# Batch 0's second half masked by multiplication, its gates reordered and one scaling moved to GpSimd, in an attention and SwiGLU kernel

## Chip, cores and metric

One core of a Trainium2 chip runs the whole program. The metric is the device time of one execution in microseconds, the median of several runs. Engines are named as in the profile: PE is TensorE, DVE is VectorE, ACT is ScalarE, POOL is GpSimd, SP is SyncE.

## What is computed

Windowed attention with a few global keys, and then a gated feed-forward block on its output. Batch is 4, heads 8, sequence 768, head size 64; keys 0 to 7 are global, and a query also sees the last 96 keys.

```python
scores = scale * q @ k.T - slope[h] * dist        # dist = 96 for a global key outside the window
a = softmax(where(is_global | is_local, scores, -1e9))
x = (a @ v) as [3072 tokens, 512]
g = x @ w_gate
out = (g / (1 + exp(-g)) * (x @ w_val)) @ w_out    # 512 -> 1536 -> 512
```

## The kernel before

The 3072 tokens are eight tiles of 384, two for each batch: tile 0 is the first half of batch 0, tile 1 its second half. For each batch the kernel makes queries and keys of head pairs transposed (qT, kT), scores by chunks of 120 keys, exponentials, then denominators and numerators for two quads of four heads, and from these x transposed (xT), four slabs of 128 features; quad g fills slabs 2g and 2g+1. For each tile the feed-forward part goes over 12 slices f of 128 hidden features: a gate (`gate_or_val(t, f, 0)`) and a value (`gate_or_val(t, f, 1)`), each four matmuls at L553, one for each slab of xT. The gate goes through tanh on ScalarE (L564) and a product on VectorE (L569, tile sl); the value is multiplied by that (L573) and gives hT. `out_part` multiplies three slices of hT by w_out (L585); four parts make 128 rows of the output.

Attention of the next half is woven into the feed-forward part of the tile before. The order is written out by hand: every engine runs its instructions in the order in which the Python code calls them. For tile 0 the list `tile0` (L805) holds gates, values and steps for the second half of batch 0; after it come the `stretches` (L813), which take each f of each tile with the steps that hang on it. Work that should wait a little is put on a list `later`, and `run_later(n)` (L255) takes n items off its head; the loop over `tile0` (L868) takes one before most gates and values, and all before a step.

There are two ways to put the position bias in. Batch 0 adds it before the exponential: `bias` (L340) multiplies a diagonal of the head's slope (slopeI) by the distances (dist), which starts the sum in PSUM, and `scores_half` (L351) adds the scores to it. The later batches multiply the exponential by a mask, exp(-slope * dist), which `make_masks` (L249) makes on ScalarE and `scores` (L375) applies on VectorE.

`both_values` (L506) makes denominators and numerators of a half for both quads, copies the numerators to SBUF on ScalarE (L518, tile ns) and puts four items on `later`: `spread_first` (the reciprocal denominators of quad 0 spread out, rb, and quad 0's two scalings), `spread` for quad 1 and its two scalings. A scaling is `scale_num` (L521, the instruction at L522): ns times rb gives a slab of xT. For batch 0 all four run on VectorE; for later batches quad 0's two run on GpSimd.

GpSimd also issues nearly all loads (weights, keys, queries, values), in the order of the calls from L611 to L700. Its issues wait for earlier transfers by semaphores of eight, used in turn. The loads of the last lines are w_out in four parts (`load_wo`, L215), batch 1's keys and queries (`load_qk`, L149), the global rows (`load_globals`, L177) and batch 1's values in seven chunks (`load_v_rest`, L167). PSUM banks are handed out in turn by `bank` and `spare`; `widen` (L847) gives tile 0's last slices four more of them, `narrow` takes these back in tile 1.

Of the kernel before, what the change touches and what calls it, by code (L numbers as in the profile page):

```python
# [37 lines left out]
def kernel(  # L38
# [110 lines left out]
    def load_qk(b, h0, h1):  # L149
        for st, src in ((kst[b], k), (qst[b], q)):  # L150
            nc.gpsimd.dma_start(
                out=st[:, h0:h1, :],
                in_=src[b, h0:h1].rearrange("h (p j) d -> p h (j d)", p=128))
# [13 lines left out]
    def load_v_rest(b, c):  # L167
        n = min(KC, S - KC * c)
        nc.gpsimd.dma_start(  # L169
            out=vSs[b][NG:NG + n, c, :, :],  # L170
            in_=v[b, :, KC * c:KC * c + n, :].rearrange("h p d -> p h d"))
# [5 lines left out]
    def load_globals():  # L177
        for dst, src in ((kG, k), (vG[:, 1:], v)):
            nc.gpsimd.dma_start(
                out=dst.rearrange("p b h d -> p (b h) d"),  # L180
                in_=src[1:, :, 0:NG, :].rearrange("b h p d -> p (b h) d"))

    def copy_globals(b, c0=0):
        nc.sync.dma_start(
            out=vSs[b][0:NG, c0:],
            in_=vG[:, b, :, :].unsqueeze(1).broadcast_to([NG, NCH - c0, H, D]))
# [28 lines left out]
    def load_wo(g):  # L215
        nc.gpsimd.dma_start(
            out=wo[:, 3 * g:3 * g + 3, :],
            in_=moe_w_out[384 * g:384 * g + 384].rearrange("(f p) d -> p f d", p=128))
# [26 lines left out]
    def single(name, tag, dt=FP32):  # L245
        return ps.tile([128, 512 if dt == FP32 else 1024], dt, name=name, tag=tag)
# [13 lines left out]
    class Pair:  # L260
# [87 lines left out]
                        start=(col == 0), stop=False, skip_group_check=True)  # L348
            return sc

        def scores_half(self, half, which, sc, put_off=False):  # L351
            hp = self.hp
            for c, col, q0, n in SCORES[half, which]:
                for hi in range(2):
                    r = slice(64 * hi, 64 * hi + 64)
                    nc.tensor.matmul(  # L356
                        sc[hi][:, col:col + n],
                        lhsT=self.kT[r, 128 * c:128 * c + 128],
                        rhs=self.qT[r, q0:q0 + n], start=False, stop=True,
                        skip_group_check=True)  # L360
            c, col, q0, n = SCORES[half, which][-1]
            at = sb2.tile([128, 2, BANK], FP16, name="at", tag=f"at{half + which}", bufs=NP)
            self.at[half, which] = at

            def exps():
                for hi in range(2):
                    nc.scalar.activation(out=at[:, hi, 0:col + n], in_=sc[hi][:, 0:col + n],  # L367
                                         func=AF.Exp, scale=scale)

            if put_off:  # L370
                later.append(exps)
            else:
                exps()

        def scores(self, bk, mul_eng, sc):  # L375
            hp = self.hp
# [129 lines left out]
    def both_values(b, half):  # L506
        two = [quads[b, g] for g in range(2)]
        for quad in two:
            den = spare("den") if b > 0 else bank("den")
            quad.weigh(half, den, None)  # L510
            quad.invert(den)
        srcs = {}
        for g, quad in enumerate(two):
            for side in range(2):
                num = spare("num") if b == 0 and g == 1 else bank("num")
                quad.weigh(half, num, side)
                src = sb2.tile([128, TB], FP32, name="ns", tag="ns", bufs=4)
                nc.scalar.copy(out=src, in_=num[:, 0:TB])  # L518
                srcs[g, side] = src

        def scale_num(eng, g, side):  # L521
            eng.tensor_mul(two[g].x_out(half, side), srcs[g, side], two[g].rb)  # L522

        def spread_first():
            two[0].spread()
            for side in range(2):
                scale_num(nc.gpsimd if b > 0 else nc.vector, 0, side)

        later.append(spread_first)
        def spread():  # L530
            two[1].spread()

        later.append(spread)
        for side in range(2):
            def scale(side=side):
                scale_num(nc.vector, 1, side)

            later.append(scale)
# [19 lines left out]
    def gate_or_val(t, f, which, c0=0):  # L558
        products(t, f, which, c0, NC)
        dst = gv.pop((f, which))  # L560

        if which == 0:
            th = sb2.tile([128, TB], FP32, name="th", tag="th")
            nc.scalar.activation(out=th, in_=dst[:, 0:TB], func=AF.Tanh, scale=0.5)  # L564
            if t == 0 and f < 4:
                sl = sb2.tile([128, TB], FP32, name="sl", tag="ns", bufs=4)
            else:
                sl = sb2.tile([128, TB], FP32, name="sl", tag="sl")
            nc.vector.scalar_tensor_tensor(  # L569
                out=sl, in0=th, scalar=1.0, in1=dst[:, 0:TB], op0=AluOp.add, op1=AluOp.mult)  # L570
            gv["sl", f] = sl
        else:
            nc.vector.tensor_mul(hTs[t][:, f, :], dst[:, 0:TB], gv.pop(("sl", f)))  # L573
# [82 lines left out]
    p_tr(1, "x2", "o0", A)  # L656
    V(out=vG[:, 0], in_=vG32)
    V(out=vSs[0][0:NG, 0:4], in_=vG[:, 0].unsqueeze(1).broadcast_to([NG, 4, H, D]))
    copy_globals(0, 4)
    load_w(wg, 0)  # L660
    load_half(1, 0, 4)
# [21 lines left out]
    quads[0, 1].denominators(single("den", "o0"))  # L683
    for side, tag in enumerate(("x2", "x0")):
        quads[0, 1].numerators(side, single("num", tag))

    load_w(wg, 8)
    for c in range(3, NCH):
# [1 line left out]
    load_w(wv, 8)  # L690
    load_wo(0)
    load_wo(1)
    load_wo(2)
    stage(1)
    load_qk(1, 0, 4)
    load_globals()
    load_wo(3)
    load_qk(1, 4, 8)
    for c in range(NCH):
        load_v_rest(1, c)  # L700

    gv["n"] = 1
    hb = [bank("gps") for _ in range(4)]
# [1 line left out]
    def first_gates(*terms):  # L705
        for c, f in terms:
            products(0, f, 0, c, c + 1, hb[f])
# [20 lines left out]
    def vas(b, half):  # L728
        return lambda: both_values(b, half)
# [18 lines left out]
    def sch(hp):  # L748
        def step():
            p = pairs[0, hp]  # L750
            scs = [p.bias(1, 0), p.bias(1, 1)]
            for which in range(2):
                p.scores_half(1, which, scs[which], which == 1 and hp != 1)
        return step

    def fetch(b, *hps):
# [41 lines left out]
    def first_val(f):  # L798
        return lambda: products(0, f, 1, 0, 2)

    V(out=dist[:, 2 * WIN:2 * WIN + 168], in_=dist[:, WIN:WIN + 168])
    V(out=dist[:, 2 * WIN + 168:], in_=dist[:, WIN:WIN + 48])
    first_gates(*[(c, f) for f in range(4) for c in range(2)])
    first_gates((2, 0), (2, 1), (2, 2), (3, 0), (3, 1), (2, 3), (3, 2), (3, 3))
    tile0 = [(0, 0), (1, 0), (2, 0), (3, 0), trh(0, 1, True), first_val(0), first_val(1),  # L805
             bias_of(0, 0), bias_of(0, 1), scores_of(0), (0, 1), (1, 1), (2, 1),
             trh(2, 3, False), sch(1), (3, 1), (4, 0), sch(2), (5, 0), (4, 1), (5, 1),
             (6, 0), (6, 1), sch(3), (7, 0), (7, 1), (8, 0), vas(0, 1), (8, 1)]

    def ff(t, f0, f1, n_out=(0,)):  # L810
        return [(t, f, n_out[(f - f0) % len(n_out)]) for f in range(f0, f1)]

    stretches = [  # L813
        (ff(0, 9, 10) + ff(0, 10, 12, (1,)), {}),
        (ff(1, 0, 6, (1, 0, 0, 1, 1, 2)) + ff(1, 6, 10, (1, 1, 1, 0)) + ff(1, 10, 12, (2,)), first(1, 1)),
        (ff(2, 0, 12, (1,)) + ff(3, 0, 12, (1,)), both(2, 1)),
        (ff(4, 0, 12, (1,)) + ff(5, 0, 12, (1,)), both(4, 2)),
        (ff(6, 0, 12, (1,)), second(6, 3)),
# [7 lines left out]
    def mask_at(t, f, which, h, c0, c1):  # L826
        after.setdefault((t, f, which), []).append(lambda: make_masks(h, c0, c1))

    spots = [(0, f) for f in (8, 9, 10, 10, 11, 11)] + [(1, f // 2) for f in range(10)]
    for n, (t, f) in enumerate(spots):  # L830
        mask_at(t, f, n % 2, n // 2, *((0, WIN), (WIN, 3 * WIN))[n % 2])
    at_step(1, 7, lambda: [copy_globals(b) for b in range(1, B)])
    for b, base, rate, v_at in ((2, 20, 2.0, (31, 32, 33, 34, 35, 36, 37)), (3, 38, 1.4, (56, 57, 58, 59, 60, 61, 62))):
        items = [(base, lambda b=b: stage_rows(b)), (base + 1, lambda b=b: load_ends(b))]
# [10 lines left out]

    outs = [(t, i, part) for t in range(NT - 1) for i in range(3) for part in range(4)]
    def widen():  # L847
        run_later(len(later))
        x, n = state["x"], gv["n"]
        state["x"] = ([state["tags"][(state["n"] + i) % 4] for i in range(4)]  # L850
                      + [x[(n + i) % 3] for i in range(3)])
        gv["n"] = 0
# [4 lines left out]
        state["n"] += 3  # L857
        gv["n"] = 0

    at_step(0, 9, widen)  # L860
    at_step(1, 2, narrow)

    def take(step_list):
# [3 lines left out]

    for item in tile0:  # L868
        if callable(item):
            take([item])  # L870
            continue
        f, which = item
        if item not in ((5, 0), (8, 1)):
            run_later(1)
        gate_or_val(0, f, which, (NC if f < 4 else 0, 2 if f < 2 else 0)[which])
        for fn in after.pop((0, f, which), []):
            fn()
# [61 lines left out]
```

## Time and profile before

| | |
|---|---|
| runs | 240.0, 240.38, 240.97 us; median 240.38 |
| the profiled execution | 241.65 us, of which the span from the first to the last instruction is 239.9 |
| clock granted to TensorE | 0.998 |
| transfers | 25.00 MB, mean 104 GB/s |
| VectorE sl, L569 | 96 instructions, mean 551 ns |
| ScalarE tanh, L564 | 96 instructions, mean 495 ns |
| scaling, L522, on VectorE and on GpSimd | 14 with median 554 ns, 10 with median 996 ns |

The profile gives for each engine its busy time, for each line and operation the number and mean time of its instructions, and the chain of waits that ended last. A timeline row has the start in microseconds from the span's start, the length, engine, line, operation, output and inputs, how many instructions were merged (x), and in brackets how long the engine stood idle before it and what ended that.

### The profile page before, as it was taken

To read this page: it belongs to the slowest core of one execution; us is meant where nothing else is said; L and a number is where in the kernel's file an instruction comes from. 1 tells how busy PE (TensorE), PEld (TensorE's weight loads), DVE (VectorE), ACT (ScalarE), POOL (GpSimd) and SP (SyncE) were. 2 spreads that over 40 slices of the span, in tenths; PEclk is the share of its full clock that TensorE was granted. 3 is DMA by queue.
4 is the path that set the end of the run, shared out by engine and by line. 5 is a ranking of instruction groups with operands and counts; after the bars stand their busy time and mean duration, and the time that the engine had idled before them with its cause. 6 is when DMAs were issued, how large, how long until landed. Compare 5 with 4: busy or idle time off the path is not lost.

```text
span 239.9 us, 6040 instructions
## 1 busy us (share of the span) xinstructions
PE 234.5 (98%) x2424; PEld 136.0 (57%) x2424; DVE 167.9 (70%) x363; ACT 128.0 (53%) x290; POOL 94.1 (39%) x113
## 2 busy tenths in 40 slices
PE   8999999999999999999999999999999999999994
PEld 4566565656555556555655556555655556555543
DVE  6688659978897678776786668776785668555530
ACT  4647775888855374376356364376356435233311
POOL 8886575668960002995072152700031223000000
PEclk9999999999999999999999999999999999999999
DMA  7999999999998538999139849930110110111022
GB/s 131 159 201 201 188 197 204 196 166 160 159 133 127 123 84 118 115 134 120 45 61 107 120 107 136 119 63 0 48 44 3 44 44 3 46 45 44 3 87 87
DMA packets 83333, 25.00 MB, mean 104 GB/s; under 512 B 72601, under 2 KB 80361, under 8 KB 83305
## 3 DMA queue, kind: packets, MB, share of 16 engines
q0 software_dynamic: 64208, 14.05, 64.0%
q1 hardware_dynamic: 18664, 10.36, 18.0%
q8 instruction: 19, 0.31, 0.6%
q10 hardware_dynamic: 432, 0.21, 0.3%
q14 instruction: 10, 0.07, 0.1%
HBM read 28.62 MB, written 6.29 MB: 146 GB/s over the span
## 4 chain that ended last, share of the span: by engine, by line
PE 92%; DMA 3%; DVE 2%; POOL 1%; ACT 1%; issue 0%; DVEq 0%; ACTq 0%; POOLq 0%
PE gps L553 26%; PE vps L553 26%; PE ops L585 25%; PE num L445 4%; PE sc L385 3%; DMA q<-in_q_dram 3%; PE den L445 2%; PE sc L345 2%; PE trs L272 1%; PE ops L601 1%; PE sc L356 1%; POOL k L118 1%; DVE sl L569 1%; DVE xT L503 1%; PE trs L298 1%
## 5 line engine op out<-in xcount | busy, mean ns | idle before, releaser
L564 ACT ACTIVATE th<-gps 128x384 f32<-128x384 f32 x96 | 47.4, 495 | 62.6 <-PE gps L553 56.6
L569 DVE SCALAR_TENSOR_TENSOR sl<-th,gps 128x384 f32<-128x384 f32 x96 | 52.8, 551 | 38.3 <-ACT th L564 37.7
L553 PE MATMUL gps<-xT,wg 128*128 128x384 f16 x384 | 78.0, 327 | 0.3 <-DVE xT L503 0.3
L553 PE MATMUL vps<-xT,wv 128*128 128x384 f16 x384 | 77.8, 326 | 0.0
L585 PE MATMUL ops<-wo,hT 128*128 128x512 f16 x276 | 73.1, 379 | 0.0
L573 DVE TENSOR_TENSOR hT<-vps,sl 128x384 f16<-128x384 f32 x96 | 53.0, 554 | 8.2 <-PE vps L553 0.5
L553 PEld LDWEIGHTS <-wg 128*128 128x128 f16 x384 | 35.6, 98 | 31.7 <-issue 2.1
L553 PEld LDWEIGHTS <-wv 128*128 128x128 f16 x384 | 37.2, 98 | 25.2
L585 PEld LDWEIGHTS <-hT 128*128 128x128 f16 x276 | 26.9, 98 | 23.7
L393 ACT ACTIVATE at<-sc 128x432 f16<-128x432 f32 x72 | 33.8, 533 | 10.2 <-PE sc L385 10.2
L522 POOL TENSOR_TENSOR xT<-ns,rb 128x384 f16<-128x384 f32 x10 | 9.8, 996 | 66.4 <-ACT ns L518 35.1
L169 POOL DMA_DIRECT2D vS<-in_v_dram x28 | 24.7, 891 | 5.3 <-DMA kst<-in_k_dram 1.9
L591 ACT ACTIVATE osb<-ops 128x512 f32<-128x512 f32 x23 | 13.7, 597 | 14.6 <-PE ops L585 14.4
L404 POOL TENSOR_TENSOR at<-at,masks 128x864 f16<-128x864 f16 x4 | 7.3, 1825 | 23.9 <-ACT at L393 19.3
L404 DVE TENSOR_TENSOR at<-at,masks 128x864 f16<-128x864 f16 x20 | 12.2, 610 | 5.6 <-ACT at L393 5.6
L518 ACT COPY ns<-num 128x384 f32<-128x384 f32 x24 | 9.8, 493 | 9.6 <-PE num L445 9.6
L192 POOL DMA_DIRECT2D kst<-in_k_dram x16 | 14.0, 886 | 1.8 <-DMA qst<-in_q_dram 1.1
L192 POOL DMA_DIRECT2D qst<-in_q_dram x16 | 13.7, 876 | 0.3 <-issue 0.3
L367 ACT ACTIVATE at<-sc 128x432 f16<-128x432 f32 (+2 forms) x32 | 11.5, 449 | 2.9 <-PE sc L356 2.9
L401 DVE TENSOR_TENSOR at<-at,masks 128x432 f16<-128x432 f16 x24 | 8.1, 378 | 4.3 <-ACT at L393 4.3
L445 PE MATMUL num<-at,vS 128*32 128x216 f16 (+6 forms) x576 | 10.9, 224 | 0.0
L455 DVE STREAM_TRANSPOSE dT<-den 128x384 f32<-128x384 f32 x16 | 9.3, 581 | 1.2 <-PE den L445 0.5
(71 smaller groups left out, 168.0 us busy)
## 6 DMA issues: line engine op xcount, KB each, us to landing
out_dram<-osb SPq DMA_DIRECT2D x23, 256.0 KB
vS<-in_v_dram POOLq DMA_DIRECT2D x24, 120.0 KB, 6.4
wg<-in_moe_w_gate_dram POOLq DMA_DIRECT2D x6, 256.0 KB, 8.8
wv<-in_moe_w_val_dram POOLq DMA_DIRECT2D x6, 256.0 KB, 7.7
wo<-in_moe_w_out_dram POOLq DMA_DIRECT2D x4, 384.0 KB, 9.3
qst<-in_q_dram POOLq DMA_DIRECT2D x16, 96.0 KB, 5.1
kst<-in_k_dram POOLq DMA_DIRECT2D x16, 90.0 KB, 5.4
kst<-in_k_dram POOLq DMA_DIRECT2D x2, 384.0 KB, 11.1
```

The costliest lines, as they stand in the source:

```text
L169: nc.gpsimd.dma_start(out=vSs[b][NG:NG + n, c, :, :], in_=v[b, :, KC * c:KC * c + n, :].rearrange("h p d -> p h d"))
L192: nc.gpsimd.dma_start(out=st[b][p0:p0 + n, h // 2, :, h % 2, :], in_=src[b, h, 0:n * J].rearrange("(t p) d -> p t d", p=n))
L367: nc.scalar.activation(out=at[:, hi, 0:col + n], in_=sc[hi][:, 0:col + n], func=AF.Exp, scale=scale)
L393: nc.scalar.activation(out=at[:, hi, :], in_=sc[hi][:, 0:BANK], func=AF.Exp, scale=scale)
L404: mul_eng.tensor_mul(at, at, m[:, :, o:o + BANK])
L445: nc.tensor.matmul(dst[r, o:o + n], lhsT=ones[:, 0:32] if side is None else vals[:, 4 * g + j, side::2], rhs=pairs[b, 2 * g + j // 2].at[c ...
L553: nc.tensor.matmul(gv[f, which][:, 0:TB], lhsT=w[:, c, 128 * f:128 * f + 128], rhs=x_of(t)[:, c, :], start=(c == 0), stop=(c == NC - 1))
L564: nc.scalar.activation(out=th, in_=dst[:, 0:TB], func=AF.Tanh, scale=0.5)
L569: nc.vector.scalar_tensor_tensor(out=sl, in0=th, scalar=1.0, in1=dst[:, 0:TB], op0=AluOp.add, op1=AluOp.mult)
L573: nc.vector.tensor_mul(hTs[t][:, f, :], dst[:, 0:TB], gv.pop(("sl", f)))
L585: nc.tensor.matmul(ops, lhsT=hTs[t][:, f, 128 * i:128 * i + 128], rhs=wo[:, f, :], start=(f == 0), stop=(f == NFF - 1))
L591: nc.scalar.mul(out=osb, in_=ops, mul=0.5)
```

## The change

Five things are changed, and the loop is fitted to them.

- Pairs 1 to 3 of batch 0's second half (`sch`) no longer call `bias`. Their score matmuls start the sum themselves, and each exponential is followed by multiplications with a mask on VectorE: two for the first part of a half (72 and 192 columns of two heads), one for the second (432 columns of two heads). Pair 0 (`bias_of`, `scores_of`) stays.
- The masks that this needs, columns WIN to 3*WIN of heads 2 to 7, are made before tile 0's first tanh; the two copies that extend dist stand further ahead. The remaining masks keep their number and get other places.
- Gates and values of tile 0 stand in another order, the list now reaches to the tile's end, two output parts are in it, and three later ones change places in tile 1. The tile sl gets three buffers. `widen` is called after `both_values` and no longer empties `later`.
- Quad 0's two scalings of batch 0's second half go to GpSimd.
- The third and fourth part of w_out, the global rows, the second half of batch 1's keys and queries and its values are called in a step of `tile0`, `late_widen`, which stands after `vas(0, 1)` and ahead of gate 10.

```diff
-        def scores_half(self, half, which, sc, put_off=False):
+        def scores_half(self, half, which, sc, put_off=False, masked=False):
...
-                        rhs=self.qT[r, q0:q0 + n], start=False, stop=True,
+                        rhs=self.qT[r, q0:q0 + n], start=masked, stop=True,
...
+            def mask():
+                for a, d0, m in BIAS[half, which]:
+                    a2 = at[:, :, a:a + m]
+                    nc.vector.tensor_mul(a2, a2, masks[:, 2 * hp:2 * hp + 2, d0:d0 + m])
...
+            if masked:
+                later.append(mask)
...
-                scale_num(nc.gpsimd if b > 0 else nc.vector, 0, side)
+                scale_num(nc.gpsimd, 0, side)
...
-                sl = sb2.tile([128, TB], FP32, name="sl", tag="sl")
+                sl = sb2.tile([128, TB], FP32, name="sl", tag="sl", bufs=3)
...
+    V(out=dist[:, 2 * WIN:2 * WIN + 168], in_=dist[:, WIN:WIN + 168])
+    V(out=dist[:, 2 * WIN + 168:], in_=dist[:, WIN:WIN + 48])
     copy_globals(0, 4)
...
+    for h in range(2, H):
+        make_masks(h, WIN, 3 * WIN)
...
-    load_wo(2)
     stage(1)
     load_qk(1, 0, 4)
-    load_globals()
-    load_wo(3)
-    load_qk(1, 4, 8)
-    for c in range(NCH):
-        load_v_rest(1, c)
+
+    def late_loads():
+        load_wo(2)
+        load_globals()
+        load_wo(3)
+        load_qk(1, 4, 8)
+        for c in range(NCH):
+            load_v_rest(1, c)
...
-            scs = [p.bias(1, 0), p.bias(1, 1)]
             for which in range(2):
-                p.scores_half(1, which, scs[which], which == 1 and hp != 1)
+                p.scores_half(1, which, banks("sc"), which == 1 and hp != 1, True)
+            if hp != 1:
+                later.insert(0, later.pop(1))
...
+    def late_widen():
+        late_loads()
+        widen()
+
+    def out_next():
+        out_part(*outs.pop(0))
+
     tile0 = [(0, 0), (1, 0), (2, 0), (3, 0), trh(0, 1, True), first_val(0), first_val(1),
              bias_of(0, 0), bias_of(0, 1), scores_of(0), (0, 1), (1, 1), (2, 1),
-             trh(2, 3, False), sch(1), (3, 1), (4, 0), sch(2), (5, 0), (4, 1), (5, 1),
-             (6, 0), (6, 1), sch(3), (7, 0), (7, 1), (8, 0), vas(0, 1), (8, 1)]
+             trh(2, 3, False), sch(1), (3, 1), (4, 0), (5, 0), sch(2), (6, 0), (4, 1), (5, 1),
+             (6, 1), sch(3), (7, 0), (7, 1), (8, 0), (9, 0), vas(0, 1), late_widen, (10, 0), (8, 1),
+             (11, 0), (9, 1), (10, 1), out_next, (11, 1), out_next]
...
-        (ff(0, 9, 10) + ff(0, 10, 12, (1,)), {}),
-        (ff(1, 0, 6, (1, 0, 0, 1, 1, 2)) + ff(1, 6, 10, (1, 1, 1, 0)) + ff(1, 10, 12, (2,)), first(1, 1)),
+        (ff(1, 0, 6, (0, 0, 0, 1, 2, 2)) + ff(1, 6, 10, (1, 1, 1, 0)) + ff(1, 10, 12, (2,)), first(1, 1)),
...
-        run_later(len(later))
         x, n = state["x"], gv["n"]
...
     for item in tile0:
         if callable(item):
-            take([item])
+            if item is not late_widen and item is not out_next:
+                run_later(len(later))
+            item()
             continue
         f, which = item
-        if item not in ((5, 0), (8, 1)):
+        if item == (8, 1):
+            run_later(3)
+        elif item not in ((6, 0), (7, 0)):
             run_later(1)
```

More of the change, by code (lines that the diff above doesn't have):

```diff
@@ L799, in first_val @@
         return lambda: products(0, f, 1, 0, 2)
-    V(out=dist[:, 2 * WIN:2 * WIN + 168], in_=dist[:, WIN:WIN + 168])
-    V(out=dist[:, 2 * WIN + 168:], in_=dist[:, WIN:WIN + 48])
     first_gates(*[(c, f) for f in range(4) for c in range(2)])
     first_gates((2, 0), (2, 1), (2, 2), (3, 0), (3, 1), (2, 3), (3, 2), (3, 3))
+    def late_widen():
[3 more added lines that the diff above has]
+        out_part(*outs.pop(0))
     tile0 = [(0, 0), (1, 0), (2, 0), (3, 0), trh(0, 1, True), first_val(0), first_val(1),
              bias_of(0, 0), bias_of(0, 1), scores_of(0), (0, 1), (1, 1), (2, 1),
-             trh(2, 3, False), sch(1), (3, 1), (4, 0), sch(2), (5, 0), (4, 1), (5, 1),
-             (6, 0), (6, 1), sch(3), (7, 0), (7, 1), (8, 0), vas(0, 1), (8, 1)]
+             trh(2, 3, False), sch(1), (3, 1), (4, 0), (5, 0), sch(2), (6, 0), (4, 1), (5, 1),
+             (6, 1), sch(3), (7, 0), (7, 1), (8, 0), (9, 0), vas(0, 1), late_widen, (10, 0), (8, 1),
+             (11, 0), (9, 1), (10, 1), out_next, (11, 1), out_next]
     def ff(t, f0, f1, n_out=(0,)):
@@ L827, in mask_at @@
         after.setdefault((t, f, which), []).append(lambda: make_masks(h, c0, c1))
-    spots = [(0, f) for f in (8, 9, 10, 10, 11, 11)] + [(1, f // 2) for f in range(10)]
-    for n, (t, f) in enumerate(spots):
-        mask_at(t, f, n % 2, n // 2, *((0, WIN), (WIN, 3 * WIN))[n % 2])
+    for h, (t, f) in enumerate(((0, 9), (0, 10), (0, 11), (1, 0), (1, 1), (1, 2), (1, 3), (1, 4))):
+        mask_at(t, f, 1, h, 0, WIN)
+    for h, f in ((0, 10), (1, 11)):
+        mask_at(0, f, 0, h, WIN, 3 * WIN)
     at_step(1, 7, lambda: [copy_globals(b) for b in range(1, B)])
@@ L858, in narrow @@
         gv["n"] = 0
-    at_step(0, 9, widen)
     at_step(1, 2, narrow)
```

## Prediction

> **What bounds the kernel now.** I read the page's busy shares and chain first, then TensorE's timeline around the end of tile 0, then GpSimd's timeline over the same stretch.
>
> ```profile
> PE 234.5 (98%) x2424; PEld 136.0 (57%) x2424; DVE 167.9 (70%) x363; ACT 128.0 (53%) x290; POOL 94.1 (39%) x113
> ...
> PE 92%; DMA 3%; DVE 2%; POOL 1%; ACT 1%; issue 0%; DVEq 0%; ACTq 0%; POOLq 0%
> ```
>
> TensorE is busy for 98% of the span and carries 92% of the chain that ends last. So every microsecond of matmul removed shortens the kernel, and every microsecond in which TensorE waits lengthens it. The question is whether a new wait appears. TensorE's timeline (start, length, line, operation) at the border of tiles 0 and 1:
>
> ```profile
> 40.24 0.81 PE L553 MATMUL vps<-xT,wv 128*128 128x384 f16 x4
> 40.89 0.81 PE L585 MATMUL ops<-wo,hT 128*128 128x512 f16 x3
> 41.53 0.81 PE L553 MATMUL gps<-xT,wg 128*128 128x384 f16 x4
> 42.18 0.81 PE L553 MATMUL vps<-xT,wv 128*128 128x384 f16 x4
> ```
>
> Four products take 0.65 us from start to start (40.24 to 40.89) and nothing stands between groups. The row at 41.53 is the first gate of tile 1, the first reader of the x of batch 0's second half (xT, written at L522). Its four matmuls read quad 0 (c = 0, 1) and quad 1 (c = 2, 3); VectorE had finished all four scalings at 40.56. Now GpSimd, whose queue issues the loads:
>
> ```profile
> 31.16 0.77 POOL L216 DMA_DIRECT2D wo<-in_moe_w_out_dram  x1 [0.16 <-DMA vS<-in_v_dram]
> 32.57 0.80 POOL L151 DMA_DIRECT2D kst<-in_k_dram  x1 [0.64 <-DVE hT L573]
> 33.59 0.75 POOL L151 DMA_DIRECT2D qst<-in_q_dram  x1 [0.22 <-ACT th L564]
> 34.83 0.68 POOL L179 DMA_DIRECT2D kG<-in_k_dram  x1 [0.49 <-issue]
> ...
> 36.16 0.78 POOL L216 DMA_DIRECT2D wo<-in_moe_w_out_dram  x1
> 37.43 0.81 POOL L151 DMA_DIRECT2D kst<-in_k_dram  x1 [0.49 <-DMA wo<-in_moe_w_out_dram]
> 39.34 0.75 POOL L151 DMA_DIRECT2D qst<-in_q_dram  x1 [1.09 <-DMA wo<-in_moe_w_out_dram]
> 41.30 0.95 POOL L169 DMA_DIRECT2D vS<-in_v_dram  x1 [1.21 <-DMA wo<-in_moe_w_out_dram]
> 43.24 0.94 POOL L169 DMA_DIRECT2D vS<-in_v_dram  x1 [1.00 <-DMA kst<-in_k_dram]
> 45.27 3.59 POOL L169 DMA_DIRECT2D vS<-in_v_dram  x4 [1.09 <-DMA qst<-in_q_dram]
> 49.47 0.64 POOL L169 DMA_DIRECT2D vS<-in_v_dram  x1 [0.61 <-DMA kst<-in_k_dram]
> ```
>
> GpSimd is late: it issues batch 1's last load at 49.47 and is free at 50.11, 8.6 us after TensorE has begun tile 1. The brackets show why: before most issues it waits for an earlier transfer to land, while the page's DMA row stands at 9 tenths in every slice from 6 to 72 us. The queue runs as fast as the transfers let it, and the place of a load in the program's text doesn't slow it or speed it.
>
> [...] L522 took 996 ns on GpSimd and 554 on VectorE, 1.8 times. [...] Here GpSimd's pool configuration is changed (two records of 44 ns) at 70.2, ahead of its first L522, but that L522 then waited for ScalarE until 94.4, so this trace neither shows nor excludes the price. [...]
>
> ```profile
> 4.38 1.19 PE L345 MATMUL sc<-dist,slopeI 128*128 128x432 f16 x6
> ...
> 11.05 0.70 PE L345 MATMUL sc<-dist,slopeI 128*128 128x432 f16 x6
> ```
>
> The same six matmuls cost 1.19 us early and 0.70 later. No long idle of TensorE stands in the trace[...].
>
> **The change, part by part.**
>
> *Bias matmuls of pairs 1 to 3 go.* Each pair had six at L345: 0.70 us from start to start for pair 1 (23.77 to 24.47), 0.69 for pair 2 (26.19 to 26.88), 0.69 for pair 3 (30.58 to 31.27). TensorE saves 2.08 us, and reaches tile 1's first gate at 41.53 - 2.08 = 39.45 if nothing in tile 0 stalls.
>
> *Mask multiplications come* on VectorE, three a pair. L404 has 610 ns for 864 elements and L401 378 for 432; the line through both gives 223 ns for 2x72 and 352 for 2x192. A pair costs 223 + 352 + 610 = 1.19 us, three 3.56. Two scalings leave (2 x 0.554 = 1.11): net 2.45 us more. From 20 to 40 us VectorE is busy 7.60 + 7.26 = 14.9 of 20, so 5.1 us are free. Bounds: nothing, or up to 2.45 us of delay to TensorE in tile 0. I take nothing, for the reason under the fourth part: a delay of tile 0 of less than 18 us is hidden there. Without that cover it would cost up to 2.45.
>
> *Six masks earlier on ScalarE* stand between the last exp and the first tanh, where it idles 3.41 us (14.69 to 18.10). A 432-wide mask is 0.55 and neighbours overlap by about 0.10 (0.38 + 0.55 alone, 0.83 as a pair), so six take 6 x 0.55 - 5 x 0.10 = 2.8. The two copies of dist (0.19 and 0.17) move into VectorE's 1.22 us of idle before 10.18. Both cost nothing; uncovered they would be hidden like the masks. Gate order, PSUM rotation, the third sl buffer and the shifted output parts keep the counts on TensorE; their new waits lie in tile 0 or leave the sum of tile 1 alone. Two output parts precede tile 1 before and after. Cost nothing, with the same cover.
>
> *Quad 0's scaling moves to GpSimd, and this decides.* The step that holds the late loads runs directly after the step that only puts the scaling on the list of postponed work. The scaling is taken off that list at the next gate. So the built program's order on GpSimd is: third wo load, kG, vG, fourth wo, second kst and qst, seven vS loads, a library reload, and only then the two scalings. The late loads are ahead of the scaling, not behind it, as the summary has it. Tile 1's first two matmuls each wait for GpSimd, and all of TensorE's queue stands behind them.
>
> When is GpSimd free? All issues before the scaling are those of before with the third wo moved behind kst and qst: the same bytes, and the last vS issue again waits for the second kst load. I take 50.11. Even if no load waited, the 13 issues take 0.77 + 0.68 + 0.66 + 0.78 + 0.81 + 0.75 + 0.95 + 0.94 + 3.59 + 0.64 = 10.57 us after about 33.4 (34.34, the end of the qst issue, less the third wo's 0.77 and 0.16): 44.0, still after 39.45. The reload has no row[...]. A gain is excluded, since an instruction is added. [...] The two scalings take 1.96 together (a pair at 94.43); add 0.1 for the signal. [...]
>
> *What follows.* Before, from that second matmul (41.53 + 0.16 = 41.69) to the end of the span took 239.9 - 41.69 = 198.2 us of dense TensorE work, and none of it is removed. TensorE will have stood still for 57.1 - 39.45 = about 18 us, and I let it restart at half rate for 4 us, which costs half of that, 2.0; bounds 0 (the clock doesn't fall) and 4.4 (as in this trace's start, where the slow rate lasted from 1.2 to about 10). The loads for batch 2, queued behind the scaling, come 8 us later, but their readers come 18 later.
>
> The sum: 58.12 + 198.2 + 2.0 = 258.3 us of span, against 239.9. The profiled execution took 241.65, 1.75 more than its span, but the median of the runs, 240.38, lies 0.48 above that span. On the median's footing: 258.8.
>
> **Rivals.** *The reload costs nothing.* For it: its records are 44 ns, and the first scaling of before took no longer than the other nine (992 to 1001 ns). Against: those had 24 us of idle in front. Then 58.12 falls to 52.17 and the median to 252.8.
>
> *The scaling goes in time (the other side).* If GpSimd came to the scaling by 39.45 - 1.96 - 0.1 = 37.4, for instance because the loads truly stood behind it, TensorE wouldn't wait and only the bias saving would stay: 240.38 - 2.08 = 238.3. Against it stands the built order, and the 10.57 us of issue work. The point from which it decides is 37.4 against 50.11.
>
> *A longer wait.* [...]
>
> **How the numbers follow.** Forecast (reload paid) 0.52, reload free 0.34, longer wait 0.09, in time 0.04, something that lands within 0.5% 0.01. The predicted time is 258.8. The range starts at the free reload less 1.5 for a clock that stays up or loads that land earlier, 251.3, and ends at 261.5, which leaves out the tail of the longest wait and the fast case. A difference under 0.5%, 1.2 us, is about what a measurement of this kernel cannot tell from no change. Slower 0.95, within it 0.01, faster 0.04.
>
> **What would show it.** On TensorE: the first gate of tile 1 reached near 39.5, its first matmul at about 57 (51 if the reload is free) waiting for GpSimd's xT. On GpSimd: the last vS issue ending near 50[...], then two scalings of about 1.0. Matmuls after the gap about 320 ns apart instead of 163 for some 4 us. From there to the end 198 us plus 2. No L345 rows for pairs 1 to 3. I am wrong if GpSimd's scaling stands before the late loads, or those are issued by 37.

## The result and the profile after

The changed kernel takes 254.53 us (median of four runs, 254.2 to 254.78), against 240.5 us for the kernel before (four runs beside it): 1.058 times as long, 95% interval 1.056 to 1.061. The profiled execution took 254.57 us, and its span is 252.8.

The page of the changed kernel: busy shares, TensorE's row and its clock row of the 40 slices (6.3 us each, in tenths), and the chain that ended last by engine.

```profile
PE 234.7 (93%) x2406; PEld 135.3 (54%) x2406; DVE 169.2 (67%) x370; ACT 127.7 (51%) x290; POOL 95.9 (38%) x115
...
PE   8799995079999999999999999999999999999995
...
PEclk9999999569999999999999999999999999999999
...
PE 78%; DMA 15%; POOL 5%; issue 1%; ACT 0%; POOLq 0%
```

TensorE has as many busy microseconds as before (234.7 against 234.5, although 18 matmuls are gone), but 93% of a longer span instead of 98%. One slice of its row, from 44 to 51 us, is 0, and in the chain DMA and POOL have taken 20% together. The clock row, all 9 before, has a 5 and a 6 at the same place.

TensorE's timeline of the changed kernel, from the last work of tile 0 to the first gates and values of tile 1:

```profile
40.48 0.81 PE L592 MATMUL ops<-wo,hT 128*128 128x512 f16 x3
51.55 0.48 PE L560 MATMUL gps<-xT,wg 128*128 128x384 f16 x1 [10.27 <-POOL xT L529]
52.50 1.12 PE L560 MATMUL gps<-xT,wg 128*128 128x384 f16 x3 [0.47 <-POOL xT L529]
53.42 1.48 PE L560 MATMUL vps<-xT,wv 128*128 128x384 f16 x4
54.70 0.96 PE L560 MATMUL gps<-xT,wg 128*128 128x384 f16 x4
55.49 0.81 PE L560 MATMUL vps<-xT,wv 128*128 128x384 f16 x4
```

The first gate of tile 1 waits 10.27 us for the first scaling on GpSimd, and its second matmul 0.47 us more for the second. Then the four products of a value take 1.28 us from start to start (53.42 to 54.70), where four took 0.65 before: the half clock. At 55.49 they are back at about 0.65. GpSimd in the same kernel:

```profile
45.45 3.58 POOL L169 DMA_DIRECT2D vS<-in_v_dram  x4 [0.99 <-DMA wo<-in_moe_w_out_dram]
49.76 0.64 POOL L169 DMA_DIRECT2D vS<-in_v_dram  x1 [0.73 <-DMA kst<-in_k_dram]
50.50 1.95 POOL L529 TENSOR_TENSOR xT<-ns,rb 128x384 f16<-128x384 f32 x2
```

The last load of batch 1 is issued until 50.40, and the scalings follow at 50.50. From the third part of w_out, at 33.52, to 50.40 the 13 issues themselves fill 10.5 us, and GpSimd waits 6.4 between them, nearly all of it for transfers; each of these waits is for the transfer issued eight places before, the last one, at 49.76, for the kst of 37.73. The scalings' inputs had been there since 36.95, when VectorE ended rb. The view of line L529 gives the shortest, median and longest time in ns, then the first and last start:

```profile
L529 POOL TENSOR_TENSOR xT<-ns,rb x12: 987/995/1004, 50.5 to 213.8; 128x384 f16<-128x384 f32 x12
...
L529 POOLq MODIFY_POOL_CONFIG  x2: 37/37/37, 50.4 to 50.4; - x2
```

What the prediction calls the library reload is the two records of 37 ns. The first scaling begins 0.1 us after them and is among the twelve that take 987 to 1004 ns: the reload cost next to nothing.

Cut at the second matmul of tile 1's first gate, the two spans compare as follows.

| us | before | after |
|---|---|---|
| TensorE goes on with tile 0's first gates, after its 0.33 wait for xT | 17.25 | 17.80 |
| from there until TensorE is ready for tile 1 | 24.28 | 23.48 |
| tile 1's second matmul starts | 41.70 | 52.50 |
| from there to the end of the span | 198.2 | 200.3 |

### The profile page after: what moved, and what is told of

It reads as the page before. It is cut to its first block, busy times and chain, and to the rows that moved or that the text cites. A ratio compares the mean times of both kernels' runs of the same rounds, so it can differ in the third digit from the quotient of the medians.

```text
span 252.8 us, 6015 instructions
## 1 busy us (share of the span) xinstructions
PE 234.7 (93%) x2406; PEld 135.3 (54%) x2406; DVE 169.2 (67%) x370; ACT 127.7 (51%) x290; POOL 95.9 (38%) x115
## 4 chain that ended last, share of the span: by engine, by line
PE 78%; DMA 15%; POOL 5%; issue 1%; ACT 0%; POOLq 0%
PE ops L592 23%; PE gps L560 23%; PE vps L560 22%; DMA kst<-in_k_dram 5%; DMA wg<-in_moe_w_gate_dram 4%; DMA wo<-in_moe_w_out_dram 3%; PE sc L392 3%; DMA wv<-in_moe_w_val_dram 3%; PE num L452 3%; PE den L452 2%; PE trs L272 1%; POOL vS L169 1%; PE ops L608 1%; POOL k L118 1%; POOL q L118 1%
## 5 line engine op out<-in xcount | busy, mean ns | idle before, releaser
L529 POOL TENSOR_TENSOR xT<-ns,rb 128x384 f16<-128x384 f32 x12 | 11.7, 995 | 79.7 <-DVE rb L468 68.7
```

## Experiments

Theory A: the scaling is late because 13 load issues stand before it in GpSimd's queue, several of them held by transfers; TensorE's pause then also lets its clock fall. Rivals: B, GpSimd itself (its speed, the reload) makes the scaling late wherever it stands; C, the masks and the new order of tile 0 lose the time; D, calling the loads late is what costs.

**The scaling ahead of all late loads**

```diff
     def late_widen():
+        run_later(1)
         late_loads()
...
-        elif item not in ((6, 0), (7, 0)):
+        elif item not in ((6, 0), (7, 0), (10, 0)):
```

> The changed kernel with one thing moved: quad 0's scaling is called before all the late loads, so that on GpSimd it stands ahead of the third w_out load. Theory A (the queue: the scaling was late because 13 load issues stood before it): the scaling runs as soon as its inputs are there, about 37 to 39 us, TensorE doesn't stop at tile 1, and what stays is the 0.8 us that tile 0 took less in the changed kernel's trace: 239.4 to 240.2. Theory B (the scaling is late because GpSimd is the slower engine for it, or because of the library reload, wherever it stands): over 243. Theory C (the masks and the new order of tile 0 lost the time): about 250. A cost of its own under A: the loads behind the scaling are issued some 5 us later, which would show as waits for kst or vS in tile 1.

Measured: 240.98 us, ratio to the kernel before 1.0004 (0.9987 to 1.002). All of the 14 us are gone with one call moved. GpSimd and then TensorE of this version:

```profile
35.95 1.96 POOL L529 TENSOR_TENSOR xT<-ns,rb 128x384 f16<-128x384 f32 x2 [2.96 <-DVE rb L468]
37.86 0.80 POOL L216 DMA_DIRECT2D wo<-in_moe_w_out_dram  x1
```

```profile
39.32 0.81 PE L592 MATMUL ops<-wo,hT 128*128 128x512 f16 x3
39.97 0.81 PE L560 MATMUL gps<-xT,wg 128*128 128x384 f16 x4
```

The same two scalings end at 37.91 and TensorE goes from tile 0 to tile 1 without a bracket. Now GpSimd waits for VectorE (2.96) instead of TensorE for GpSimd. The loads behind it begin later, but the last vS issue starts at 49.23 here and at 49.76 in the changed kernel: the transfers set that moment. B falls, and C falls as the cause of the 14 us. The time is 0.8 us above what A expected, which the mended versions below take up.

**The scaling between the late loads**

```diff
         load_wo(3)
+        run_later(1)
         load_qk(1, 4, 8)
```

(and the same second edit as above)

> The changed kernel with quad 0's scaling between the fourth w_out load and the second half of batch 1's keys: GpSimd comes there at about 36.6, just before the scaling's inputs are ready (36.95). Theory A: as with the scaling first, 239.4 to 240.2, and the loads behind it only 1 to 2 us later than in the changed kernel. Theory B: over 243. Theory C: about 250.

Measured: 241.0 us, ratio 1.0007 (0.9995 to 1.0019). GpSimd waits 0.71 us for rb instead of 2.96 and the time is the same, so the loads' delay shows no cost in either place.

**The scaling back on VectorE**

```diff
-                scale_num(nc.gpsimd, 0, side)
+                scale_num(nc.gpsimd if b > 0 else nc.vector, 0, side)
```

> The changed kernel with quad 0's scaling back on VectorE, the late loads as in the change. Theory A: no stop at tile 1; VectorE has 1.1 us more before tile 1's first gate, where it had ended at 41.9 with its last hT at the time TensorE came (41.3), so 239.4 to 240.5. Theory B: the same. Theory C: about 250. Theory D (calling the loads late is itself what costs): over 243.

Measured: 240.82 us, ratio 0.9998 (0.9984 to 1.0012). Calling the loads late shows no cost (D falls), and the rest of the change brings nothing either.

**The scaling on GpSimd alone**, in the kernel before:

```diff
-                scale_num(nc.gpsimd if b > 0 else nc.vector, 0, side)
+                scale_num(nc.gpsimd, 0, side)
```

> The kernel before with one edit: quad 0's scaling of batch 0's second half on GpSimd, the loads called where they were. Theory A: GpSimd reaches the scaling at about 50.1 all the same, TensorE stops at 41.5 and goes on at about 52.1 with the second matmul, then 198.2 us and 1.2 to 2 for the slow clock: 252.4 to 253.2, which is 12 to 12.7 more than before. Theory C: no more than 1 or 2 us over before. Theory D: as before.

Measured: 253.93 us, ratio 1.0538 (1.0508 to 1.0567). One edit of one line has nearly the whole loss, 13.2 of about 14 us; the time is 0.7 above what A expected. GpSimd and TensorE of this version:

```profile
48.92 0.64 POOL L169 DMA_DIRECT2D vS<-in_v_dram  x1 [0.74 <-DMA kst<-in_k_dram]
49.66 1.96 POOL L522 TENSOR_TENSOR xT<-ns,rb 128x384 f16<-128x384 f32 x2
```

```profile
39.66 0.81 PE L585 MATMUL ops<-wo,hT 128*128 128x512 f16 x3
50.71 0.48 PE L553 MATMUL gps<-xT,wg 128*128 128x384 f16 x1 [10.24 <-POOL xT L522]
```

It is the picture of the changed kernel: last vS issue, scalings, and a wait of 10.24 us. The second matmul of the gate starts at 51.66, and from there to the end this trace takes 252.2 - 51.66 = 200.5 us, 2.3 more than the 198.2 of the kernel before, with the same work in the same order on TensorE. Theory A is shown from both sides: the scaling behind the loads makes the loss by itself, and taking it out from behind them removes it.

**TensorE kept busy through the pause**

```diff
+    def keep_busy(n):
+        rest = single("rest", state["x"][gv["n"] % len(state["x"])])
+        for _ in range(n):
+            nc.tensor.matmul(rest[:, 0:256], lhsT=ones[:, 0:128], rhs=ones[:, 0:256],
+                             start=True, stop=True)
...
+    keep_busy(80)
     for tiles, steps in stretches:
```

> The changed kernel with 80 matmuls of 256 columns on ones, whose results nobody reads, queued on TensorE between tile 0 and tile 1's first gate[...]. Theory A (the pause ends when GpSimd's scalings end, and what follows it is slower for a while because the clock fell): the pause's end stays where it is, the matmuls after it run at 163 ns instead of some 310 at once, and the kernel gets 1.2 to 1.5 us faster than the changed one, about 253.2. Rival: the slow matmuls after the pause have another cause[...]: no change, 254.5.

Measured: 254.19 us, ratio 1.0553 (1.0525 to 1.0581): no change that can be told from the 1.0583 of the changed kernel, where theory A expected about 253.2. The trace says why, so this run decided nothing:

```profile
39.38 8.90 PE L889 MATMUL rest<-ones 128*128 128x256 f16 x80
50.90 0.45 PE L560 MATMUL gps<-xT,wg 128*128 128x384 f16 x1 [2.62 <-POOL xT L529]
...
52.76 1.49 PE L560 MATMUL vps<-xT,wv 128*128 128x384 f16 x4
```

The added matmuls end 2.62 us before the gate, and even so the value at 52.76 takes 1.28 us (to 54.04): the 2.62 us were long enough for the clock to fall (0.99 from 48 to 51 us, 0.50 from 51 to 54). It took more of them:

```diff
-    keep_busy(80)
+    keep_busy(100)
```

> As the run kept busy with 80 matmuls, with 100 of them: at 0.11 us each they fill 11.0 of the 11.5 us that TensorE stands still, so less than 1 us of pause is left where 2.6 us were, and after those 2.6 us the clock had fallen all the same. Theory A (the slow matmuls after the pause are the fallen clock): now the clock stays up, the first products run at 163 ns, and the time is 1.0 to 1.4 us below the changed kernel run beside it. Rival (another cause, such as the loads under way): they stay slow and the time stays within 0.4.

> The changed kernel as it is, beside the run that keeps TensorE busy to the end of the pause, so that both stand against the same runs of the kernel before: 254.0 to 255.0 under every theory.

Measured: 252.58 us, ratio 1.051 (1.0492 to 1.0528), and the changed kernel beside it 255.52 us, ratio 1.0606 (1.0579 to 1.0632). That is 1 us more than at its first measurement and half a microsecond above the expected range; its five runs lie between 253.79 and 255.58. The two differ by 2.9 us, more than the 1.0 to 1.4 that theory A expected. The windows view (stretch, length, busy time with instructions for PE, PEld, DVE, ACT and POOL, granted clock, DMA share, GB/s) for the first work of tile 1, first of the changed kernel, then of the one kept busy to the end:

```profile
48.00:51.00 3.00, 0.00 (x0) 0.00 (x0) 0.00 (x0) 0.00 (x0) 2.18 (x4) 0.50 1.81 178
51.00:54.00 3.00, 1.98 (x6) 0.80 (x6) 0.00 (x0) 0.34 (x1) 3.00 (x5) 0.50 2.40 150
```

```profile
48.00:51.00 3.00, 3.00 (x30) 2.70 (x28) 0.00 (x0) 0.00 (x0) 2.16 (x3) 1.00 1.87 176
51.00:54.00 3.00, 2.40 (x16) 1.24 (x15) 0.45 (x1) 0.76 (x2) 3.00 (x5) 1.00 2.42 148
```

The column before the last two is the clock: 0.50 late in the pause and after it, against 1.00. TensorE in the version kept busy to the end:

```profile
52.83 0.81 PE L560 MATMUL vps<-xT,wv 128*128 128x384 f16 x4
53.48 0.81 PE L560 MATMUL gps<-xT,wg 128*128 128x384 f16 x4
```

With the clock up, four products after the pause take 0.65 us (52.83 to 53.48), though the transfers are as busy (2.40 and 2.42 from 51 to 54 us). So the slow products are the clock, and the rival falls. From tile 1's second matmul to the end this version has 251.4 - 52.34 = 199.1 us, the changed kernel 200.3 in its first trace and 253.7 - 52.80 = 200.9 in its second: the fallen clock costs 1.2 and 1.8 us there, and the 2.3 us of the scaling alone are of the same kind. Of the 2.9 us between the two times, 1.8 stand after that matmul in the two traces, and 0.5 before it, since the changed kernel's pause ended later (52.80 against 52.34). The rest is not taken apart.

**The masks alone**, in the kernel before: no bias matmuls for pairs 1 to 3, their masks and multiplications as in the change.

```diff
-            scs = [p.bias(1, 0), p.bias(1, 1)]
             for which in range(2):
-                p.scores_half(1, which, scs[which], which == 1 and hp != 1)
+                p.scores_half(1, which, banks("sc"), which == 1 and hp != 1, True)
+            if hp != 1:
+                later.insert(0, later.pop(1))
```

> The kernel before with the masks alone: pairs 1 to 3 without bias matmuls, multiplied by masks that are made ahead of tile 0's tanh; order of gates, loads, scalings and output parts as before. If the 2.08 us of bias matmuls are a pure saving for TensorE: 238.7. If VectorE's 3.6 us of multiplications come too late for the denominators of quad 1, as the 0.6 us wait for L373 in the traces of the runs so far suggests, 1 to 1.5 of it are lost: 239.5 to 240.3. A loss against before would need a wait of over 2 us at the denominators: over 241.

Measured: 241.05 us, ratio 1.0018 (1.0005 to 1.0032). Nothing is gained, and I had expected 239.5 to 240.3. TensorE at the denominators, first in the kernel before, then in this version:

```profile
33.73 0.79 PE L445 MATMUL den<-at,ones 128*32 128x72 f16 x40
...
35.68 0.82 PE L553 MATMUL vps<-xT,wv 128*128 128x384 f16 x4
```

```profile
31.60 1.09 PE L452 MATMUL den<-at,ones 128*32 128x72 f16 x30
33.40 0.34 PE L452 MATMUL den<-at,ones 128*32 128x216 f16 x8 [0.70 <-DVE at L373]
...
34.92 0.82 PE L560 MATMUL vps<-xT,wv 128*128 128x384 f16 x4
```

Denominators and numerators take 34.92 - 31.60 = 3.32 us here and 35.68 - 33.73 = 1.95 in the kernel before: 1.37 of the 2.08 saved are spent there, on waiting for masks, though the bracket shows only 0.70 (a row that waits in its middle has the rest in its length). 0.28 more go to a wait for wv that the earlier arrival meets, and the remainder is not taken apart. From the same first matmul of tile 0 to tile 1's first gate it is 24.29 us, against 24.28 before.

**Two waits mended.** The version with the scaling first, with pair 3's scores one place earlier, and the output parts of tile 1 redistributed:

```diff
-             (6, 1), sch(3), (7, 0), (7, 1), (8, 0), (9, 0), vas(0, 1), late_widen, (10, 0), (8, 1),
+             sch(3), (6, 1), (7, 0), (7, 1), (8, 0), (9, 0), vas(0, 1), late_widen, (10, 0), (8, 1),
...
-        (ff(1, 0, 6, (0, 0, 0, 1, 2, 2)) + ff(1, 6, 10, (1, 1, 1, 0)) + ff(1, 10, 12, (2,)), first(1, 1)),
+        (ff(1, 0, 6, (0, 0, 0, 2, 1, 2)) + ff(1, 6, 10, (1, 1, 1, 0)) + ff(1, 10, 12, (2,)), first(1, 1)),
```

> The version with quad 0's scaling ahead of the late loads, and two edits against the waits that its trace shows: pair 3's scores go before value 6 instead of after it (so its masks come earlier than the denominators of quad 1, which waited 0.62 us for them), and tile 1's output parts come as 2, 1, 2 instead of 1, 2, 2 at slices 3 to 5 (so no part 0 comes directly after a part 3, where it waited 0.69 us for ScalarE to empty the bank). If the bias saving was eaten by these two waits and what goes with them: 1.3 to 1.8 us below the version with the scaling first, 239.2 to 239.7. If it was lost elsewhere: no change, 241.

Measured: 239.77 us, ratio 0.9969 (0.9955 to 0.9982): the lowest of all versions, 0.3% below the kernel before. The version with the scaling first was 1.2 us slower, but each stands against other runs of the kernel before (medians 240.62 and 240.76); by the ratios, 0.9969 and 1.0004, the gain is about 0.8 us. The wait for the output bank that it removes, as it stands in the version with the scaling first:

```profile
48.68 0.81 PE L592 MATMUL ops<-wo,hT 128*128 128x512 f16 x3
50.18 0.81 PE L592 MATMUL ops<-wo,hT 128*128 128x512 f16 x3 [0.69 <-ACT osb L598]
```

Part 0 of the next output rows comes directly after part 3 of the last ones, in the same bank, and ScalarE first has to empty that, which takes it 0.60 us from the end of part 3 on (49.53 to 50.13). Tile 1 takes 31.51 us there (first gate to first gate), 30.68 in the kernel before and 30.77 in the mended version. Both waits are gone from its trace, but tile 0 is no shorter: until TensorE is ready for tile 1 it takes 23.68 us, against 23.53 in the version with the scaling first and between 23.3 and 24.1 in the seven traces that have the new order with these scores where they were. What stands in tile 0 instead is

```profile
PE gps L560 <- DMA wg<-in_moe_w_gate_dram: 0.4, 1, 0.4
```

This row has the total, the number and the longest of the waits. So what the trace shows as gained is tile 1's 0.74 us, from the order of the output parts; that taking away the wait for the masks saved anything is not shown.

**The second denominators later.** The output parts mended as above, the scores left where they were, and in batch 0 the denominators of quad 1 after the numerators of quad 0:

```diff
-        for quad in two:
-            den = spare("den") if b > 0 else bank("den")
-            quad.weigh(half, den, None)
-            quad.invert(den)
+        def turn(quad):
+            den = spare("den") if b > 0 else bank("den")
+            quad.weigh(half, den, None)
+            quad.invert(den)
+
+        for quad in two[:2 if b > 0 else 1]:
+            turn(quad)
...
+            if b == 0 and g == 1:
+                turn(quad)
```

> The same with the output parts mended, but the wait for the masks met in another way: pair 3's scores stay after value 6, and in batch 0 the denominators of quad 1 are computed after the numerators of quad 0, 0.6 us later. If the wait for the masks is one of order alone: as the other mended version, 239.2 to 239.7. If VectorE's load as a whole is the limit in tile 0: TensorE waits later for an L576 or L580 instead, and it stays within 0.3 of 240.3.

Measured: 240.08 us, ratio 0.998 (0.9968 to 0.9993): also a little below the kernel before. The time lies in the range of the second theory, but the sign that it named is not there: no wait for the masks (L373) is left and no new one for VectorE's products of gates and values, but one for a load:

```profile
PE num L452 <- DMA vS<-in_v_dram: 0.8, 1, 0.8
```

Quad 0's numerators, now ahead of quad 1's denominators, meet a load of values that isn't there yet. Tile 0 takes 23.69 us and tile 1 30.82, much as in the other mended version. In both the longest new wait in tile 0 is for a load; that the transfers are the next limit there is likely, but no run tests it.

## Why the prediction was right

- *GpSimd is free at 50.11, whatever the change of the calls.* Right: 50.40. That the late loads stand ahead of the scaling decided the sign, and the runs with the scaling first, between and alone show it.
- *The price of the reload.* This is the term that was mis-sized: 0.1 us from the last issue to the first scaling, in the changed kernel and in the run with the scaling alone. The rival with the free reload, to which I gave 0.34 against 0.52, is what happened; the range held because it was drawn to take in both. No trace showed the price that the forecast counts, and the runs show none beyond the 0.1. Whether anything was loaded at all, no run tells. The signal, put at 0.1, took 0.04: the second scaling ends at 52.46 and the gate's second matmul starts at 52.50.
- *The slow clock, 2.0 us.* Right in kind, and 1.2 to 2.3 in size: 1.2 and 1.8 in the two traces of the changed kernel, 2.3 in that of the scaling alone. That the clock would fall, and stay down for 4 us, was an assumption of mine that no trace had shown; it was at 0.50, and for 3.4 to 5.7 us of the work after the pause.
- *The 198.2 us of the rest.* 199.1 with the clock kept up. I had put the shifted output parts at nothing; they cost 0.83 in tile 1, shown by its length with and without them. From the second matmul to the end the forecast had 200.2 and the trace 200.3, but that is luck: 0.8 too much for the clock and 0.83 too little for the output parts cancel.
- *TensorE reaches tile 1 at 39.45.* It was 41.28: the trace started tile 0 0.55 later, and 1.28 of the 2.08 were lost; tile 0's denominators and numerators, where the wait for the masks stands, account for 0.88 of that (2.83 us against 1.95). As predicted the pause hid that; the bound that I gave for it uncovered, up to 2.45, holds. The 0.55 can't be put down to the change: its second trace starts tile 0 at 16.40, earlier than the 17.25 of the kernel before.
- *On the median's footing, 0.48 above the span.* Here I chose badly. The time of a profiled execution lies 1.75 above its span in the kernel before and 1.77 in the changed one; I set the one execution's span against the median of others.

The point forecast was 4.3 us too high. The clock gave some 0.8 too much; the output parts, the footing and 0.3 of GpSimd's delay gave 0.8, 1.3 and 0.3 too little. The rest of the difference is the price of the reload, which was not shown. On its own terms the free-reload rival, 252.8, was 1.7 too low, of which 1.3 is the footing.

The second question is where the 2.08 us of bias matmuls went once the pause is taken away. The version with the scaling first has 23.53 us in tile 0 instead of 24.28 and 31.51 in tile 1 instead of 30.68, while the span after that is the same to 0.02. So 1.3 us are lost in tile 0, of which 0.88 stand where TensorE waits for the masks, and 0.83 at the output bank. The second loss is mended by the order of the output parts, and 0.2 to 0.3% of the kernel's time stays gained in the two versions that have it. The first is not mended: with the wait for the masks gone, a wait for a load comes in its place and tile 0 is as long as before the mending.

## What to carry to other kernels

An operation moved to an engine that also issues loads gets the place in that engine's queue where it is called, behind every load called before it and each of their waits: here the same two scalings started at 50.50 us behind 13 loads and at 35.95 ahead of them. Look when the queue comes free (50.40), and not how long the operation takes there (1.95). An operation that is only put on a list of postponed work isn't on any queue yet, and a load called after that step still goes ahead of it, as all 13 did here. Matmuls that are removed count only as far as the work that replaces them comes in time for the next reader, and as the loads that the following work needs have landed: of the 2.08 us removed here, the version with the masks alone gained nothing (ratio 1.0018).

## What the runs showed of the hardware that was not expected

- A pause of 2.6 us, after 8.9 us of dense matmuls, was enough for TensorE's clock to be at 0.5 when it went on. A shorter one was enough as well: in the trace of the scaling between the late loads, TensorE waits 1.45 us for a load of q until 9.86 us; from 10 to 13 us the granted clock is 0.50 (0.993 over the whole execution, against 1.000 with the scaling first), and six matmuls at L345 take 1.19 us, where six took 0.70 before the pause. In the version with the scaling first a pause of 1.10 us near the same place left them at 0.70. In the changed kernel's two traces the clock had fallen 3.5 and 2.5 us after the last matmul. What decides between 1.10 and 1.45 us, no run tells.
- Once TensorE went on, the half clock lasted from 3.4 us (changed kernel, 51.55 to 54.99) to 5.7 us (scaling alone, 50.71 to 56.45).
- At the start of most traces the matmuls run at half rate while the clock row shows full speed: the first six at L345 take 1.10 to 1.19 us in ten of twelve traces, and 0.84 and 0.70 in the two others. How long this lasts differs from trace to trace of the same program. In the profiles of the kernel before and of the changed kernel the second six are still slow (1.19 us, at 7.88 and 8.50), and tile 0 starts at 17.25 and 17.80; in the nine traces in which the second six take 0.70 and the clock stays up, it starts between 15.7 and 16.6. So the start of tile 0 in one trace says little about a change.
- The two records of pool configuration ahead of GpSimd's first scaling took 37 ns each in the changed kernel, and the scaling began 0.1 us after the first of them.
